# Two batches' forward transform kept on chip by transposes, and the second batch written ahead of the expert blocks

## The chip, the cores and the metric

One core of one Trainium2 chip. The metric is the device time of one execution in microseconds. PE is the tensor engine, DVE the vector engine, ACT the scalar engine, POOL the GpSimd engine; SP issues the plain DMAs from one queue, POOL the indirect ones.

## What is computed

Each of 8 batches (2496 x 256) is filtered along its length by a product in the frequency domain. The result, 19968 tokens of 256 numbers, goes through a mixture of 8 experts, each token to the two with the highest noisy logits.

```python
X = np.fft.rfft(x, axis=1)
y = np.fft.irfft(X * (filt_r + 1j * filt_i), n=2496, axis=1)      # x: 8 x 2496 x 256
x = y.reshape(19968, 256)
noisy = x @ w_gate + np.log1p(np.exp(x @ w_noise)) * noise        # 19968 x 8
# top 2 per token; weights = softmax of the two
out[mask] += w[mask, k, None] * (np.maximum(x[mask] @ w1[e], 0) @ w2[e])   # w1: 256 x 1024
```

## The kernel before

The length 2496 is split as 39 x 64, so that both transforms are small products with constant matrices. A batch has 22 groups of rows; a half-batch (n = 0 to 15) is one batch at 128 of the 256 channels. The steps, each with its function:

- `s1l` loads two groups of x (234 KB). `s1` multiplies by the 39-point matrix (`rC`, line 247: one f32 product of 512 columns for the first batches). `s1e` copies the result `c1` and writes it to memory, `fd` (line 264).
- `kgl` reads `fd` back as `fx` with frequency on the partitions (line 271, two DMAs of 128 KB for each of five groups `kg` of a half-batch). `kg0` passes it on or splits it into a high and a low part. `kg1` multiplies by the 64-point matrix (`rM`, line 292) and then by the filter (`fr`, `fi`; lines 302 to 305, four DVE instructions). `kg2` is the inverse 64-point product (line 316) and its copy into `G`.
- `logit_half` (line 328), `logits`, `gating` and the generator `gate` work out the gates, and with them, for each token, the place in the experts' lists (DVE, with small pieces on POOL).
- `t3` transposes `G` (line 379), `i2` does the inverse 39-point product (lines 394 to 396, three products of a split operand) and writes the tokens to `y` in memory (line 400).
- `route` writes the token numbers to the experts' lists, 44 indirect DMAs of POOL per batch (line 685).
- An expert block of 512 tokens reads its list (`lt`, line 703), gathers tokens (`xg`, line 722), loads and splits weights (`wst`, lines 753, 776, 777), turns the tokens (`turn`, line 736) and does both products (lines 113 to 115 into `hps` and `yps`); POOL adds the result to the output (line 835).

`load_filter` brings half of `fr` or `fi`, in four pieces over the prelude; every filter row is wanted twice, on partitions 0 to 63 and 64 to 127, and is loaded by a DMA with a broadcast leading dimension:

```python
t[:, h, k].rearrange("p k d -> p (k d)"),
io[nm][:, h, k].rearrange("b k d -> b (k d)").unsqueeze(0).to_broadcast([2, QB, n])
```

`sign` then multiplies `fi` by a table on POOL (line 205). `setup2` loads the remaining constants, `init_dram` and `zero_out` clear lists and output.

The order of the work: `fft_stream` is a generator that writes the transform of all batches; at each `yield` it may be left. It first writes batch 0 to its gates, then the inverse of batch 0 with the first stage of batch 1, and from n = 2 on, half-batch by half-batch, the forward steps X of n beside the inverse steps Y of n - 1. A yielded number says which batch is routed. `run` takes the stream to the first routed batch, then writes expert blocks and lets the stream advance in step with them (`PACE`), 2 blocks with batch 0 and 6 with batch 1. A scheduler reorders what has been written by a timing model, engine by engine. While `early` holds, the transform borrows the experts' buffers (tags such as `hh`, `wst`, `w1h`) and PSUM banks (`EARLY`).

Of the kernel before, what the change touches and what calls it, by code (L numbers as in the profile page):

```python
# [20 lines left out]
QA, QB = 39, 64  # L21
# [37 lines left out]
def _tables():  # L59
# [48 lines left out]
    sgn = np.concatenate([sg, -sg], 0).astype(np.float32)  # L108
    return dict(cf=cf, cm=np.ascontiguousarray(big[:, :248]).astype(np.float32), hl=hl, kf=kf, sgn=sgn, tok=tok, ok=tb < QB, small=small, lin=lin)

# [13 lines left out]
LEAD = 6  # L124
EARLY = {"q1": ("hps", 2), "q5": ("yps", 2), "q6": ("yps", 2), "u1": ("xps", 1)}


class Moe:
# [18 lines left out]
    def setup(self):  # L147
        tc, nc, io, cp = self.tc, self.nc, self.io, self.cp
        self.z = cp.tile([128, D], F32, name="z")
        nc.gpsimd.memset(self.z, 0.0)  # L150
        self.ident = cp.tile([128, 128], F32, name="ident")
        make_identity(nc, self.ident)
        self.cV = cp.tile([128, 128], F32, name="cf")
        hl = cp.tile([128, 732], R32, name="hl")
        self.small = cp.tile([128, 512], F32, name="small")
        self.fr = cp.tile([128, 2, 20, 128], F32, name="fr")
        self.fi = cp.tile([128, 2, 20, 128], F32, name="fi")
        self.wg = cp.tile([128, 2, 32], F32, name="wg")
        self.sgn = cp.tile([128, 20], F32, name="sgn")
        cm = self.P.tile([128, 248], F32, name="cm", tag="mxh0", bufs=1)  # L160
        nc.sync.dma_start(cm[:, 0:120], io["cm"][:, 0:120])
        with self.after(self.s1l(0, 0)):
            nc.sync.dma_start(cm[:, 120:248], io["cm"][:, 120:248])
        nc.sync.dma_start(self.cV, io["cf"])
        nc.sync.dma_start(self.sgn, io["sgn"])
        self.rC, self.rM = cm[:RP, 0:120], cm[:, 120:248]
# [12 lines left out]
        self.nblk = cp.tile([E, 1], F32, name="nblk")  # L179
        for t in (self.cnt, self.done, self.nblk):  # L180
            nc.vector.memset(t, 0.0)
        self.tab = cp.tile([1, 2, SW], F32, name="tab")

    def setup2(self):
        nc, io, hl = self.nc, self.io, self.hl
        for a in range(0, 732, 366):
            t = self.P.tile([128, 366], F32, name="cl", tag="fx", bufs=2)
            nc.sync.dma_start(t, io["hl"][:, a:a + 366])
            nc.scalar.copy(hl[:, a:a + 366], t)
        nc.sync.dma_start(self.small, io["small"])  # L190
        nc.sync.dma_start(self.wg[:, :, 0:16], io["wgn"])
        nc.vector.tensor_copy(self.base, self.eoff)

    def load_filter(self, h, a, b):
        nc, io = self.nc, self.io
        k, n = slice(4 * a, 4 * b), 512 * (b - a)
        for t, nm in (self.fr, "fr"), (self.fi, "fi"):

            self.lastx = nc.sync.dma_start(
                t[:, h, k].rearrange("p k d -> p (k d)"),  # L200
                io[nm][:, h, k].rearrange("b k d -> b (k d)").unsqueeze(0).to_broadcast([2, QB, n]))

# [35 lines left out]
    def s1(self, bt, g0):  # L238
# [19 lines left out]
        self.s1e(bt, g0, q)  # L258

    def s1e(self, bt, g0, q):  # L260
        nc, P, early = self.nc, self.P, self.early
# [24 lines left out]
    def kg1(self, n, kg):  # L286
# [6 lines left out]
        else:  # L293
            nc.tensor.matmul(p, Mh, th, start=True, stop=False)
            nc.tensor.matmul(p, Mh, tl, start=False, stop=False)
            nc.tensor.matmul(p, Ml, th, start=False, stop=True)
        a = P.tile([128, 4, 128], F32, name="a", **(dict(tag="wst", bufs=4) if self.early else dict(bufs=2)))
        b = P.tile([128, 4, 128], F32, name="b", bufs=1)
        p3 = p.rearrange("p (k d) -> p k d", k=4)
# [4 lines left out]
        nc.vector.tensor_mul(b[64:128], p3[0:64], fi[0:64])  # L304
        nc.vector.tensor_add(a, a, b)
        self.zz[n, kg] = a
# [66 lines left out]
    def t3(self, n, g0):  # L373
# [6 lines left out]
        m = 128 * k  # L380
        th = P.tile([128, 512], R32, name="th", **(dict(tag="w1h", bufs=4) if self.early else dict(bufs=3)))
        tl = P.tile([128, 512], R32, name="tl", **(dict(tag="w1l", bufs=4) if self.early else dict(bufs=3)))
        nc.scalar.copy(th[:120, :m], q[:120, :m])
# [3 lines left out]
    def i2(self, n, g0):  # L387
# [5 lines left out]
        p = self.ps("q6")  # L393
        nc.tensor.matmul(p[:RP, :m], Dh, th[:120, :m], start=True, stop=False)
        nc.tensor.matmul(p[:RP, :m], Dh, tl[:120, :m], start=False, stop=False)
        nc.tensor.matmul(p[:RP, :m], Dl, th[:120, :m], start=False, stop=True)
        yt = P.tile([RP, 4, 128], F32, name="yt", **(dict(tag=("mxl0", "mxh1", "mxl1")[g0 // 4 % 3], bufs=1) if self.early else dict(bufs=2)))
# [4 lines left out]
    def fft_stream(self):  # L402
# [10 lines left out]
        def s1(j):  # L413
            ahead(min(j + 5, 11) if j < 11 else j + 5 if self.early else j + 2)
            self.s1(*todo[j])

# [12 lines left out]

        more(self.load_filter, 0, 0, 2)  # L430
        q = [(n, kg) for n in range(2) for kg in range(5)]
        for t in range(13):
            if t < 10:
                self.kgl(*q[t])
                self.sign(*q[t])
            if t == 0:
                more(self.load_filter, 0, 2, 5)
            if t == 3:
                more(self.load_filter, 1, 0, 2)
                more(self.setup2)  # L440
            if t == 5:
                more(self.load_filter, 1, 2, 5)
            if t == 8:
                ahead(15)
            if 2 <= t < 12:
                self.kg0(*q[t - 2])
                self.kg1(*q[t - 2])
            if t >= 3:
                self.kg2(*q[t - 3])
            if t == 9:  # L450
                self.logit_half(0, 0)
# [24 lines left out]
        self.i2(1, gs[5])  # L476
        for i in range(4):
            more(self.zero_out, 0, i)
        for _ in range(4):
            self.gating_more(0)  # L480
        yield -1
        ns = 22
        route = self.route(0, *self.routes.pop(0))
        for n in range(2, N + 1):
            X = []
# [11 lines left out]
            if m >= 2:  # L497
                Y += [f(self.logit_half, m, 0), f(self.logit_half, m, 1)]
                T = [f(self.t3, m, g) for g in gs]
                I = [f(self.i2, m, g) for g in gs]  # L500
                if m % 2:
                    Y += [f(self.logits, 0), f(self.logits, 1), T[0], f(self.gating, m // 2)]
# [13 lines left out]
            for t in range(tot):  # L516
                while ix < len(X) and ix * tot <= t * len(X):
                    X[ix]()
                    ix += 1
                    if n == 2:  # L520
                        next(route, None)
                    yield -1
# [183 lines left out]
    def front(self, blk, xg):  # L706
# [3 lines left out]
        with self.after(self.spw):  # L710
            re = nc.sync.value_load(tabi[0:1, 1, s:s + 1], min_val=0, max_val=E - 1)
        w1st, w2st = self.load_w(re, "w1", nt), self.load_w(re, "w2", nt)
        w1 = [self.wsplit(w1st[q], "w1", q) for q in range(4)]
        return w1, self.turn(xg, nt), w2st

    def gather(self, blk, i):
# [3 lines left out]
        for t in range(nt):  # L720
            x = self.P.tile([128, D], F32, name="xg", bufs=8)
            self.nc.gpsimd.indirect_dma_start(  # L722
# [22 lines left out]
    def load_w(self, re, nm, nt):  # L745
# [3 lines left out]
        if nt == BLK // 128:  # L749
            r = []  # L750
            for q in range(4):
                t = P.tile([128, 1, 512], F32, name="wst", bufs=4)
                self.spw = nc.sync.dma_start(t, src[:, q].rearrange("e p f -> p e f"))
                r.append(t[:, 0])
            return r
        self.wodd = 1 - self.wodd if nm == "w1" else self.wodd
        if nm == "w2" and self.wodd:
            r = [P.tile([128, 1, 512], F32, name="wst", bufs=4) for _ in range(4)]
            for q in range(4):
                self.spw = nc.sync.dma_start(r[q], src[:, q].rearrange("e p f -> p e f"))  # L760
            return [t[:, 0] for t in r]
        if nm == "w2":
# [24 lines left out]
    def expert(self, parts, may):  # L787
# [5 lines left out]
        while self.ahead:  # L793
# [32 lines left out]
            for t in range(nt):  # L826
                p = self.PS.tile([128, D], F32, name="yps", bufs=2)
                for f in range(8):
# [3 lines left out]
                         start=(f == 0), stop=(f == 7))  # L832
                o = P.tile([128, D], F32, name="yo", bufs=6)
                nc.scalar.activation(o, p, AF.Copy, scale=gate[:, t, 1:2])  # L834
# [107 lines left out]
```

## Time and profile before

| | |
|---|---|
| median of 3 runs | 2489.76 us (2489.31 to 2491.03) |
| the profiled execution | 2490.21 us, its span 2488.3 us |
| PE busy | 2252.4 us, 91% of the span |
| VectorE, ScalarE, GpSimd busy | 1319.8, 1202.2, 1235.0 us |
| mean granted PE clock | 0.953 |

PE busy counts the time in which at least one matmul is under way; the granted clock is the share of full speed that PE was given. The rows of instructions in order of time give the start, the length, the engine (with a q where its queue issues a DMA), the line, output <- inputs, the count, and in brackets the idle time before and what ended it. The rows of a stretch give busy time (and instructions) of each engine, the granted clock, the mean busy share of the 16 DMA engines and what they moved.

### The profile page before, as it was taken

Reading aid. Unit: us, or ns where it says so; the run is one execution under the profiler, and the core shown is the slowest. Engines: PE = TensorE matmul, PEld = TensorE weight load, DVE = VectorE, ACT = ScalarE, POOL = GpSimd, SP = SyncE. Lnnn points to the kernel's source line nnn. Section 1 sums busy time; section 2 is a strip of 40 time slices with the busy share of each in tenths; the row PEclk is TensorE's granted clock in tenths of the full one; section 3 lists DMA queues with packets and bytes.
Section 4 is the critical chain, followed back from the end, with each engine's and each line's share of the span. In section 5 each row is a group of like instructions: output and inputs, shape, how many; then the busy total and the mean of one; then the engine's idle time right before and its main releaser. Section 6 shows DMA issues by size and latency. Waiting matters only on the chain.

```text
span 2488.3 us, 41972 instructions
## 1 busy us (share of the span) xinstructions
PE 2252.4 (91%) x14769; PEld 1974.4 (79%) x14769; DVE 1319.8 (53%) x2567; ACT 1202.2 (48%) x2274; POOL 1235.0 (50%) x1065
## 2 busy tenths in 40 slices
PE   2265796998998999999998999999999999999998
PEld 0133575887887888888887899989889989999998
DVE  0237775776666667576643434334334334456775
ACT  1144564564555555555543434344344344456775
POOL 0005375574574346533665467657744444444442
PEclk6687898999999999999998999999999999999999
DMA  4274657766656565455343443443444444558774
GB/s 137 78 226 133 184 130 196 185 154 166 154 125 164 139 152 146 114 150 148 92 91 77 95 94 78 105 91 86 97 91 96 90 92 94 137 139 221 227 236 99
DMA packets 300288, 330.34 MB, mean 133 GB/s; under 512 B 48310, under 2 KB 215598, under 8 KB 300072
## 3 DMA queue, kind: packets, MB, share of 16 engines
q1 hardware_dynamic: 227368, 243.30, 32.4%
q0 software_dynamic: 72704, 84.31, 20.3%
q8 instruction: 118, 1.93, 0.3%
q14 instruction: 98, 0.80, 0.1%
HBM read 220.33 MB, written 108.43 MB: 132 GB/s over the span
## 4 chain that ended last, share of the span: by engine, by line
PE 63%; DMA 2%; POOL 2%; DVE 2%; issue 1%; ACT 1%; SPq 0%; ACTq 0%; POOLq 0%; DVEq 0%
PE yps L113 9%; PE yps L115 9%; PE yps L114 9%; PE hps L113 9%; PE hps L114 9%; PE hps L115 9%; PE xps L736 2%; PE q L316 1%; POOL lst L685 1%; PE hq L115 1%; PE hq L114 1%; PE hq L113 1%; PE q L379 1%; POOL out L835 1%; DMA fd<-c 0%
## 5 line engine op out<-in xcount | busy, mean ns | idle before, releaser
L814 DVE SCALAR_TENSOR_TENSOR hl<-hps,hh 128x512 fp32r<-128x512 f32 (+1 forms) x640 | 417.0, 656 | 564.3 <-ACT hh L813 561.7
L113 PE MATMUL yps<-w2h,hh 128*128 128x256 f32 x2560 | 701.8, 284 | 2.6 <-ACT hh L813 2.6
L835 POOL DMA_INDIRECT out<-yo,lt x320 | 521.6, 1630 | 337.2 <-ACT yo L834 255.6
L114 PE MATMUL yps<-w2l,hh 128*128 128x256 f32 x2560 | 686.3, 278 | 0.0
L115 PE MATMUL yps<-w2h,hl 128*128 128x256 f32 x2560 | 632.0, 279 | 0.7 <-DVE hl L814 0.7
L722 POOL DMA_INDIRECT xg<-y,lt x320 | 324.2, 1013 | 562.8 <-PE xps L736 407.2
L813 ACT ACTIVATE hh<-hps 128x512 fp32r<-128x512 f32 (+1 forms) x640 | 363.1, 574 | 319.6 <-PE hps L115 314.5
L115 PEld LDWEIGHTS yps<-w2h,hl 128*128 128x128 f32 x2560 | 471.5, 188 | 35.5 <-DVE hl L814 1.2
L113 PEld LDWEIGHTS yps<-w2h,hh 128*128 128x128 f32 x2560 | 483.1, 189 | 16.3 <-ACT hh L813 4.7
L113 PE MATMUL hps<-mxh,w1h 128*128 128x512 f32 (+1 forms) x1280 | 486.3, 389 | 9.0 <-DVE hl L814 6.7
L114 PE MATMUL hps<-mxl,w1h 128*128 128x512 f32 (+1 forms) x1280 | 493.8, 386 | 0.0
L114 PEld LDWEIGHTS yps<-w2l,hh 128*128 128x128 f32 x2560 | 482.2, 188 | 7.8
L115 PE MATMUL hps<-mxh,w1l 128*128 128x512 f32 (+1 forms) x1280 | 487.6, 381 | 0.0
L685 POOL DMA_INDIRECT lst<-pay,dst x352 | 363.3, 1032 | 110.0 <-issue 103.4
L834 ACT ACTIVATE yo<-yps,lt 128x256 f32<-128x256 f32 x320 | 142.8, 475 | 338.8 <-PE yps L115 173.6
L115 PEld LDWEIGHTS hps<-mxh,w1l 128*128 128x128 f32 x1280 | 241.0, 188 | 46.6
L113 PEld LDWEIGHTS hps<-mxh,w1h 128*128 128x128 f32 x1280 | 240.7, 189 | 44.7 <-DVE hl L814 13.0
L114 PEld LDWEIGHTS hps<-mxl,w1h 128*128 128x128 f32 x1280 | 241.8, 189 | 24.8
L777 DVE TENSOR_TENSOR w1l<-wst,w1h 128x512 fp32r<-128x512 f32 x172 | 118.2, 687 | 103.9 <-ACT w1h L776 103.5
L776 ACT CAST w1h<-wst 128x512 fp32r<-128x512 f32 x172 | 106.4, 620 | 126.7 <-PE hps L114 74.7
L777 DVE TENSOR_TENSOR w2l<-wst,w2h 128x512 fp32r<-128x512 f32 x208 | 135.4, 687 | 56.3 <-ACT w2h L776 55.7
L740 ACT CAST mxh<-xps 128x512 fp32r<-128x512 f32 (+1 forms) x178 | 97.2, 546 | 129.2 <-PE xps L736 80.3
(165 smaller groups left out, 2579.0 us busy)
## 6 DMA issues: line engine op xcount, KB each, us to landing
wst<-w SPq DMA_DIRECT2D x380, 256.0 KB
fd<-c SPq DMA_DIRECT2D x88, 240.0 KB
x<-x SPq DMA_DIRECT2D x88, 234.0 KB
fx<-fd SPq DMA_DIRECT2D x160, 128.0 KB
y<-yt SPq DMA_DIRECT2D x80, 234.0 KB
wb<-w SPq DMA_DIRECT2D x18, 1024.0 KB
out<-z SPq DMA_DIRECT2D x24, 702.0 KB
wc<-w SPq DMA_DIRECT2D x36, 256.0 KB
```

The costliest lines, as they stand in the source:

```text
L113: nc.tensor.matmul(o, lh, rh, start=start, stop=False)
L114: nc.tensor.matmul(o, lh, rl, start=False, stop=False)
L115: nc.tensor.matmul(o, ll, rh, start=False, stop=stop)
L685: s = nc.gpsimd.indirect_dma_start(out=self.lst, out_offset=bass.IndirectOffsetOnAxis(ap=dst[:n, i, g:g + 1], axis=0), in_=pay[:n, g, i], ...
L722: self.nc.gpsimd.indirect_dma_start(out=x, out_offset=None, in_=self.y[:BLK + ready * ROWS], in_offset=bass.IndirectOffsetOnAxis(ap=lt[:, ...
L740: nc.scalar.copy(h, q[:, :w])
L776: nc.scalar.copy(h, sv)
L777: nc.vector.tensor_sub(l, sv, f32v(h))
L813: nc.scalar.activation(h, p, AF.Relu)
L814: nc.vector.scalar_tensor_tensor(l, p, 0.0, f32v(h), op0=ALU.max, op1=ALU.subtract)
L834: nc.scalar.activation(o, p, AF.Copy, scale=gate[:, t, 1:2])
L835: a = nc.gpsimd.indirect_dma_start(out=self.io["out"][:BLK + ready * ROWS], out_offset=bass.IndirectOffsetOnAxis(ap=ids[:, t, 0:1], axis=0 ...
```

## The change

The first stage of batches 0 and 1 (`s1c`) makes x the stationary operand, so that the result has channels on the partitions, and keeps it in SBUF as `F`, one array per half of the channels. `kgc` takes the place of `kgl` and `kg0`: four PE transposes and a copy by ACT. `fd` is not written or read for these batches. Each filter load becomes two DMAs of 64 partitions, and all of them and `setup2` are written ahead of the first `kgc`. For n < 2 the addition of line 305 goes to POOL. While `early` holds, `t3` makes one f32 copy and `i2` one f32 product with an unsplit matrix (`rD`).

In the stream, after batch 0's inverse, the forward steps of n = 2 and 3 are written with the first stage of batch 2 and `route(0)`, then the inverse of n = 2 and the whole gating of batch 1, and only then comes the first yielded batch; the loop over n starts at 4. `F` shares its 22.5 KB per partition (`stage`) with the experts' `wst`, `xg` and `yo`, which are now slots of this one tile, in turn (`slot`), 4, 8 and 6 as before. In `front` w2's loads are written after w1's splits.

```diff
-EARLY = {"q1": ("hps", 2), "q5": ("yps", 2), ...
+EARLY = {"q1": ("hps", 2), "q2": ("hps", 2), "q5": ("yps", 2), ...
+        self.stage = cp.tile([128, 5632], F32, name="stage")
+        self.F = [self.stage[:, 2560 * h:2560 * h + 2560].rearrange("p (k b) -> p k b", k=CB) for h in range(2)]
+    def slot(self, nm):
+        at, n, w = {"wst": (0, 4, 512), "xg": (2048, 8, 256), "yo": (4096, 6, 256)}[nm]
+        i = self.turns[nm] = (self.turns.get(nm, -1) + 1) % n
+        return self.stage[:, at + w * i:at + w * i + w]
...
-            self.lastx = nc.sync.dma_start(
-                t[:, h, k].rearrange("p k d -> p (k d)"),
-                io[nm][:, h, k].rearrange("b k d -> b (k d)").unsqueeze(0).to_broadcast([2, QB, n]))
+            src = io[nm][:, h, k].rearrange("b k d -> b (k d)")
+            for r in range(2):
+                self.lastx = nc.sync.dma_start(t[64 * r:64 * r + 64, h, k].rearrange("p k d -> p (k d)"), src)
...
+    def s1c(self, bt, j):
+        x = self.xx.pop((bt, 2 * j))
+        if j % 2 == 0:
+            self.sq = [self.ps("q1") for _ in range(2)]
+        for h in range(2):
+            q = self.sq[h][:, :12 * CB].rearrange("p (k b) -> p k b", b=12)
+            for i in range(2):
+                o, n = 6 * (j % 2) + 3 * i, 3 if 2 * j + i < NG - 1 else 1
+                nc.tensor.matmul(q[:, :, o:o + n].rearrange("p k b -> p b k"), x[:, i * D + h * 128:i * D + h * 128 + 128],
+                                 self.rC[:, :n * CB], start=True, stop=True)
+            if j % 2 or j == 10:
+                n = 12 if j % 2 else 4
+                (nc.vector.tensor_copy if h else nc.scalar.copy)(self.F[h][:, :, 12 * (j // 2):12 * (j // 2) + n], q[:, :, :n])
+    def kgc(self, n, kg):
+        q = self.ps("q2")
+        for j in range(4):
+            nc.tensor.transpose(q[:, j * 128:j * 128 + 128],
+                                F[:, 8 * kg + 2 * j:8 * kg + 2 * j + 2].rearrange("p r b -> p (r b)"), self.ident)
+        f = self.P.tile([128, 512], F32, name="fx", tag="hl", bufs=8)
+        nc.scalar.copy(f, q)
+        self.tt[n, kg] = f, None
...
-        nc.vector.tensor_add(a, a, b)
+        (nc.gpsimd if n < 2 else nc.vector).tensor_add(a, a, b)
...
+        if tl is None:
+            nc.tensor.matmul(p[:RP, :m], self.rD, th[:120, :m], start=True, stop=True)
...
+        for a in (0, 0, 2), (0, 2, 5), (1, 0, 2), (1, 2, 5):
+            more(self.load_filter, *a)
+        more(self.setup2)
...
+        route = self.route(0, *self.routes.pop(0))
+        Y = [f(self.logit_half, 2, 0), f(self.logit_half, 2, 1), f(self.t3, 2, gs[0])]
+        for t in range(12):
+            if t < 10:
+                self.kgc(*q[10 + t])
+            if 1 <= t < 11:
+                self.kg1(*q[10 + t - 1])
+            if t >= 2:
+                self.kg2(*q[10 + t - 2])
+            for _ in range(4):
+                next(route, None)
+            if t < 11:
+                s1(22 + t)
+            if t < 4:
+                more(self.zero_out, 0, t)
+            for _ in range(3 if t >= 7 else 0):
+                if Y:
+                    Y.pop(0)()
+        self.logit_half(3, 0)
+        self.logit_half(3, 1)
+        self.logits(0)
+        self.logits(1)
+        self.gating(1)
...
+        for _ in range(10):
+            self.gating_more(1)
+        ns = 33
+        yield 0
+        for n in range(4, N + 1):
```

More of the change, by code (lines that the diff above doesn't have):

```diff
@@ L124 @@
 LEAD = 6
-EARLY = {"q1": ("hps", 2), "q5": ("yps", 2), "q6": ("yps", 2), "u1": ("xps", 1)}
+EARLY = {"q1": ("hps", 2), "q2": ("hps", 2), "q5": ("yps", 2), "q6": ("yps", 2), "u1": ("xps", 1)}
 class Moe:
@@ L296, in kg1 @@
             nc.tensor.matmul(p, Ml, th, start=False, stop=True)
-        a = P.tile([128, 4, 128], F32, name="a", **(dict(tag="wst", bufs=4) if self.early else dict(bufs=2)))
-        b = P.tile([128, 4, 128], F32, name="b", bufs=1)
+        a = P.tile([128, 4, 128], F32, name="a", **(dict(tag="w2h", bufs=4) if self.early else dict(bufs=2)))
+        b = P.tile([128, 4, 128], F32, name="b", **(dict(tag="w2l", bufs=4) if self.early else dict(bufs=1)))
         p3 = p.rearrange("p (k d) -> p k d", k=4)
@@ L380, in t3 @@
         m = 128 * k
-        th = P.tile([128, 512], R32, name="th", **(dict(tag="w1h", bufs=4) if self.early else dict(bufs=3)))
-        tl = P.tile([128, 512], R32, name="tl", **(dict(tag="w1l", bufs=4) if self.early else dict(bufs=3)))
+        if self.early:
+            t = P.tile([128, 512], F32, name="tf", tag="w1h", bufs=4)
+            nc.scalar.copy(t[:120, :m], q[:120, :m])
+            self.t3t[n, g0] = t, None
+            return
+        th = P.tile([128, 512], R32, name="th", bufs=3)
+        tl = P.tile([128, 512], R32, name="tl", bufs=3)
         nc.scalar.copy(th[:120, :m], q[:120, :m])
@@ L414, in s1 @@
             ahead(min(j + 5, 11) if j < 11 else j + 5 if self.early else j + 2)
-            self.s1(*todo[j])
+            if j < 22:
+                self.s1c(j // 11, j % 11)
+            else:
+                self.s1(*todo[j])
         def ahead(to):
@@ L428, in fft_stream @@
             yield -1
-        more(self.load_filter, 0, 0, 2)
-        q = [(n, kg) for n in range(2) for kg in range(5)]
-        for t in range(13):
+        q = [(n, kg) for n in range(4) for kg in range(5)]
+        for a in (0, 0, 2), (0, 2, 5), (1, 0, 2), (1, 2, 5):
+            more(self.load_filter, *a)
+        more(self.setup2)
+        for t in range(12):
             if t < 10:
-                self.kgl(*q[t])
+                self.kgc(*q[t])
                 self.sign(*q[t])
[L436 to L442, printed above, removed]
-            if t == 8:
[L444 to L450, printed above, removed]
+            if t == 7:
+                ahead(15)
+            if 1 <= t < 11:
+                self.kg1(*q[t - 1])
+            if t >= 2:
+                self.kg2(*q[t - 2])
+            if t == 8:
                 self.logit_half(0, 0)
@@ L476, in fft_stream @@
         self.i2(1, gs[5])
-        for i in range(4):
-            more(self.zero_out, 0, i)
         for _ in range(4):
@@ L519, in fft_stream @@
                     ix += 1
-                    if n == 2:
-                        next(route, None)
                     yield -1
@@ L720, in gather @@
         for t in range(nt):
-            x = self.P.tile([128, D], F32, name="xg", bufs=8)
+            x = self.slot("xg")
             self.nc.gpsimd.indirect_dma_start(
@@ L751, in load_w @@
             for q in range(4):
-                t = P.tile([128, 1, 512], F32, name="wst", bufs=4)
-                self.spw = nc.sync.dma_start(t, src[:, q].rearrange("e p f -> p e f"))
-                r.append(t[:, 0])
+                t = self.slot("wst")
+                self.spw = nc.sync.dma_start(t.unsqueeze(1), src[:, q].rearrange("e p f -> p e f"))
+                r.append(t)
             return r
@@ L757, in load_w @@
         if nm == "w2" and self.wodd:
-            r = [P.tile([128, 1, 512], F32, name="wst", bufs=4) for _ in range(4)]
+            r = [self.slot("wst") for _ in range(4)]
             for q in range(4):
-                self.spw = nc.sync.dma_start(r[q], src[:, q].rearrange("e p f -> p e f"))
-            return [t[:, 0] for t in r]
+                self.spw = nc.sync.dma_start(r[q].unsqueeze(1), src[:, q].rearrange("e p f -> p e f"))
+            return r
         if nm == "w2":
@@ L832, in expert @@
                          start=(f == 0), stop=(f == 7))
-                o = P.tile([128, D], F32, name="yo", bufs=6)
+                o = self.slot("yo")
                 nc.scalar.activation(o, p, AF.Copy, scale=gate[:, t, 1:2])
```

40 lines of the change are left out of this document (28 added, 12 removed).

## The prediction, made before the result was known

> **What bounds the kernel now.** I read the page's strip of 40 slices first, then one table of busy time by stretch whose cuts I chose after reading the order of instructions in time, then that order itself for the vector, DMA and tensor queues around the cuts.
>
> ```profile
> span 2488.3 us, 41972 instructions
> PE   2265796998998999999998999999999999999998
> core 0: us, PE busy (x) PEld busy (x) DVE busy (x) ACT busy (x) POOL busy (x), PEclk, DMA share, GB/s
> 0.00:20.00 20.00, 12.82 (x22) 4.07 (x22) 0.37 (x8) 7.72 (x12) 1.15 (x9) 1.00 0.81 261
> 20.00:136.00 116.00, 16.95 (x52) 10.05 (x52) 16.78 (x28) 6.66 (x7) 7.11 (x8) 0.56 0.24 80
> 136.00:170.00 34.00, 30.80 (x141) 16.18 (x141) 15.17 (x23) 19.14 (x31) 3.19 (x4) 0.89 0.82 247
> 170.00:206.00 36.00, 17.87 (x75) 10.26 (x72) 19.50 (x74) 13.62 (x28) 1.88 (x7) 0.75 0.88 268
> 206.00:264.00 58.00, 37.23 (x190) 24.53 (x194) 38.50 (x64) 27.07 (x41) 44.90 (x44) 0.82 0.36 91
> 264.00:282.00 18.00, 10.07 (x42) 5.71 (x32) 10.38 (x22) 10.48 (x22) 8.25 (x10) 0.69 0.86 264
> 282.00:372.00 90.00, 84.25 (x514) 70.07 (x514) 71.24 (x160) 54.99 (x95) 47.77 (x48) 0.97 0.52 141
> 372.00:402.00 30.00, 9.08 (x51) 5.97 (x50) 7.01 (x13) 6.04 (x10) 20.64 (x20) 0.60 0.61 146
> 402.00:2488.30 2086.30, 2033.36 (x13695) 1827.54 (x13695) 1140.85 (x2179) 1056.48 (x2031) 1100.12 (x919) 0.99 0.53 130
> ```
>
> From 402 us on, PE is busy for 2033.36 of 2086.30 us: what reaches that point earlier ends earlier, one for one. Ahead of it PE idles for 183 of 402 us. The worst stretch is 20 to 136: PE busy 16.95 of 116 us, and the DMA engines at 0.24 of their time, 80 GB/s, though 261 and 268 GB/s are reached on either side. So something slow on few engines is being waited for, not bandwidth:
>
> ```profile
> 20.06 0.74 SPq L199 DMA_DIRECT2D fr<-fr  x1
> 39.90 33.41 SPq L271 DMA_DIRECT2D fx<-fd  x6
> 44.50 2.04 POOL L205 TENSOR_TENSOR fi<-fi,sgn 128x512 f32<-128x512 f32 x2 [42.76 <-DMA fi<-fi]
> 135.99 3.03 POOL L205 TENSOR_TENSOR fi<-fi,sgn 128x512 f32<-128x512 f32 x3 [33.57 <-DMA fi<-fi]
> L205 POOL TENSOR_TENSOR fi<-fi,sgn 128x512 f32<-128x512 f32 x10 | 10.1, 1038 | 127.1 <-DMA fi<-fi 127.1
> ```
>
> The first 1 MB of filters (fr and fi, 512 KB each) is issued at 20.06 and lets the sign product go only at 44.50: 24 us. The last quarter is there at 135.99. Behind each filter load in SP's one queue stand the reads fx<-fd, six of which take 33.41 us to issue. The filter loads, with the trip of the spectrum through memory between them, set this stretch. After it a chain runs whose ends the next rows give:
>
> ```profile
> 169.46 0.81 PE L328 MATMUL u<-G,wg 128*32 128x360 f32 x8
> 205.74 1.19 POOL L685 DMA_INDIRECT lst<-pay,dst  x1 [3.03 <-DVE en L651]
> 263.28 0.89 POOL L685 DMA_INDIRECT lst<-pay,dst  x1 [0.30 <-issue]
> 281.56 1.22 PE L113 MATMUL hps<-mxh,w1h 128*128 128x512 f32 x2 [1.01 <-ACT mxh L740]
> 262.59 2.62 PE L328 MATMUL u<-G,wg 128*32 128x360 f32 x16 [4.59 <-ACT G L317]
> 314.72 1.02 POOL L685 DMA_INDIRECT lst<-pay,dst  x1 [0.31 <-DVE new L650]
> 378.69 0.90 POOL L685 DMA_INDIRECT lst<-pay,dst  x1 [0.30 <-issue]
> 391.77 0.48 PE L736 MATMUL xps<-ident,xg 128*128 128x128 f32 x1 [18.48 <-DMA xg<-y,lt]
> ```
>
> First batch: last logits of the spectrum 169.46, gates, 44 scatters of the route 205.74 to 264.2 on POOL, lists and gathers, first expert matmul 281.56. That is 112.1 us from logits to expert. Second batch: logits 262.59, route 314.72 to 379.6, and PE has nothing for 18.48 us because the gathers wait for it.
>
> **The change part by part.** The instruction prices, at full clock unless said:
>
> ```profile
> 7.35 10.78 PE L247 MATMUL q<-x,cm 117*120 117x512 f32 x20 [0.63 <-DMA x<-x]
> 79.46 1.91 PE L316 MATMUL q<-cf,a 128*128 128x128 f32 x8
> 82.67 1.13 PE L316 MATMUL q<-cf,a 128*128 128x128 f32 x8
> 83.64 1.02 PE L292 MATMUL q<-fx,cm 128*128 128x512 f32 x2
> 151.21 0.60 PE L379 MATMUL q<-ident,G 128*120 128x128 f32 x4
> 183.72 1.10 PE L379 MATMUL q<-ident,G 128*120 128x128 f32 x4 [2.52 <-DVE tl L384]
> 149.57 0.48 PE L394 MATMUL q<-th,hl 120*117 120x512 f32 x1
> 150.12 0.39 PE L396 MATMUL q<-th,hl 120*117 120x512 f32 x1
> L263 ACT COPY c<-q 120x512 f32<-120x512 f32 x46 | 27.1, 589 | 46.5 <-PE q L247 46.2 <-ACT th L383 0.3
> L317 ACT COPY G<-q 128x512 f32<-128x512 f32 x30 | 34.8, 1159 | 96.1 <-PE q L316 96.1
> L302 DVE TENSOR_TENSOR a<-q,fr 128x512 f32<-128x512 f32 x30 | 20.6, 686 | 110.4 <-PE q L292 107.8 <-PE q L296 2.0
> fd<-c SPq DMA_DIRECT2D x88, 240.0 KB
> ```
>
> *First stage (s1c).* One f32 product of 512 columns per pair of groups (10.78 us for ten) becomes four of 120 columns; nearest row L316, four f32 products of 128 columns in 1.13. Eleven make 12.4 us. Two PSUM banks are filled by two steps and then copied, one by ACT and one by DVE (0.59 by L263): the next pair waits about 0.6 us, five times, 3 us. Begun at about 5 us, the first two at half clock (1.91), it ends at 22 us, against 18 now. The writes fd<-c go, and their places in SP's queue.
>
> *Filter loads.* Each broadcast becomes two plain loads of 64 partitions, 16 issues of some 0.5 us, and none has an fx read ahead of it: they follow the last x load, about 15 us. They move 5.24 MB (fr and fi, 128 x 5120 f32 each). Their new rate stands in no row of that form; bounds are 80 GB/s (the stretch 20 to 136) and 261 (0 to 20). I take 261, since x<-x too is a plain load of one row per partition: 20 us, landing from about 19 to 37 us, the quarters in the order in which they are used. At 80 GB/s the last lands at 81. The Trainium skill, "DMA: Bandwidth & Descriptors", section "Why a DMA increments its semaphore by 16 and not by 1", says that a transfer is spread over the largest number of engines up to 16 that divides the slowest dimension of both sides: that is 2 for a broadcast whose outer dimension is 2, and 16 for 64 rows. The low share of 0.24 agrees; by the rule the sum is the one I take, and by the rate of the present loads it is rival A's.
>
> *Spectrum of the first batch (kgc, kg1, kg2).* Ten groups, each on PE four transposes (0.60), a product (1.02), eight instructions of L316 (1.13): 2.75 us. The chain of one group is the product, three DVE products (3 x 0.686), the addition, now on POOL (1.04 like L205's), then kg2; with one other group between in PE's order that sets about 3.1 us a group. ACT needs 0.59 + 1.16, POOL 2.08 with the sign product: both fit. Ten groups 31 us and 3 for the first to fill: logits at 56 instead of 169.46, **113.5 us sooner**. Bounds: 50 us (PE alone, 2.75), and 93 with the slow filters.
>
> *Gates, route, gathers of the first batch.* No instruction of it changes: 112.1 us, of which 58.4 are POOL's scatters. First expert at 168. Beside it PE now has the second batch's s1c (12.4), inverse of three half-batches (18 t3 groups, 9.9; 16.5 products of 1.02, 16.8), ten groups of 2.75 (27.5), eleven s1 (11.2) and logits, 5: 83 us in 112, where the table shows 65 busy in 170 to 282. So the transposes and the f32 product in i2 (1.02 for 0.94) cost nothing while this chain covers them; uncovered, ten times 0.60, eleven s1c at +0.05 and 17 products at +0.08 cost 8 us. zero_out, init_dram and the first y writes go past SP in this stretch; at 247 to 268 GB/s there is room, since 22 of the fd writes (5.4 MB) and as much read back as fx are gone.
>
> *Second batch's gates ahead of all blocks.* In the present kernel these gates are written between the instructions of the first blocks, and 52 us pass from logits (262.59) to the first scatter (314.72); the first batch needs 36.3. I keep the logits 19 us ahead of the first expert, as now, and take 36 to 39: the route begins 13 us sooner, and the 18.48 us wait shrinks by **13 us**. Bounds: the wait goes whole, 18.5, or grows by 10 if POOL's out additions are served first. If this wait goes, PE itself is next.
>
> *Steady part.* wst, xg and yo become slots of one tile with as many places as their pools; w2's loads are written after w1's splits, whose slots they need anyway. I take 0, bounds -10 and +10, a fifth of the 53 us that PE idles after 402.
>
> Sum against the profiled execution, 2490.2 us (span 2488.3 and 1.9 around it): 2490.2 - 113.5 - 13 = 2363.7. The median of the runs shown is 0.4 lower, so **2364**.
>
> **The rivals.** *A, filters stay slow.* The last quarter lands at 81 (80 GB/s) where the eighth group asks for it at 22 + 7 x 3.1 = 44: 37 us more, 2401. The broadcast is gone, which speaks against it.
>
> *B, cold clock and a longer chain.* PE's granted clock was 0.56 in the idle stretch and 0.82 in 206 to 264. If it stays near half through the prelude, a group costs 1.10 + 2.04 + 1.91 = 5 us, 19 us more over ten, and the 83 us beside the route become 150 or so, over 112 by some 30: about 2410. For it: four transposes took 1.10 at 183.72 after a wait. Against it: the 0.60 of others at 151.21, amid dense work. The Trainium skill, "TensorE: Matmul & The Clock Gate", section "Part 4: PE-mode transpose", says that the full clock does not engage for transposes, which would speak against adding 80 of them; the 0.60 contradicts it where products stand beside them.
>
> *C, slower.* Slots of one tile could be ordered as one thing: a weight load would wait for the last reader of any slot.
>
> ```profile
> L835 POOL DMA_INDIRECT out<-yo,lt x320 | 521.6, 1630 | 337.2 <-ACT yo L834 255.6
> 47.67 0.69 DVE L302 TENSOR_TENSOR a<-q,fr 128x512 f32<-128x512 f32 x1 [46.47 <-PE q L292]
> 73.35 0.54 SPq L199 DMA_DIRECT2D fr<-fr  x1
> ```
>
> There are 320/4 = 80 blocks; from 126.5/80 = 1.6 us a block it eats the gain, and with one addition's 1.63 us per token tile (four a block) it costs 521, a time of 2885. Against it: the product at 47.67 read a part of fr before another part's load was issued at 73.35, so parts are ordered apart.
>
> *D, no change.* The first expert sooner, but every microsecond handed back as waits for the second batch's lists: about 2490. Against it, that its forward work has 29 us of PE to spare above.
>
> **How the numbers follow.** Forecast 0.65 (2330 to 2395), A 0.08, B 0.18, C 0.05, D 0.04. Range 2330 to 2418: it takes in A and most of B, and the forecast's bounds (50 instead of 56, all of the wait, 10 in the steady part: 2342; a little more for a shorter chain). About 0.2% (5 us) is what the measurement can tell from no change: faster 0.91, same 0.03, slower 0.06.
>
> **What would show it.** Right: sign products released by 40 us, the logits at about 56, POOL's first scatter at 92, first expert at 168, the second wait under 8 us, PE nearly full after. Wrong: DMA share below 0.4 between 20 and 60 (A); granted clock below 0.8 between 20 and 150 (B); waits of weight loads on gathers or additions (C); PE idle for tens of microseconds ahead of the second batch's blocks (D).

## The result and the profile after

The changed kernel takes 2402.65 us (median of 4 runs, 2401.66 to 2403.85), the kernel before beside it 2490.4 (2489.31 to 2491.68): a ratio of 0.965 (95% interval 0.9637 to 0.9662), 88 us less. The forecast was 2364 in a range of 2330 to 2418: faster, and 39 us too low. The forecast's own span ended at 2395; the time lies in the part of the range that was added for the rivals A and B. The profiled execution took 2401.66 us, its span is 2399.9.

The table of stretches of the changed kernel, cut at its own landmarks (first expert 200, second batch's lists 262), in the columns of the table of before:

```profile
20.00:44.00 24.00, 15.30 (x72) 10.27 (x71) 8.91 (x16) 9.22 (x15) 12.59 (x13) 0.86 0.98 249
44.00:80.00 36.00, 35.82 (x246) 26.36 (x246) 17.84 (x28) 21.94 (x34) 10.23 (x9) 1.00 0.70 221
80.00:112.00 32.00, 21.86 (x92) 11.98 (x89) 16.32 (x70) 15.82 (x32) 2.08 (x7) 0.82 0.73 220
112.00:170.00 58.00, 41.05 (x200) 23.25 (x200) 39.19 (x79) 28.95 (x45) 44.90 (x44) 0.85 0.32 84
170.00:201.00 31.00, 15.71 (x59) 11.19 (x60) 19.55 (x64) 10.62 (x19) 18.16 (x24) 0.63 0.54 165
201.00:262.00 61.00, 57.82 (x356) 48.87 (x354) 43.21 (x69) 38.52 (x69) 46.08 (x42) 0.99 0.57 137
262.00:282.00 20.00, 16.65 (x103) 14.83 (x104) 11.05 (x17) 10.95 (x21) 14.21 (x13) 0.85 0.90 268
282.00:2399.90 2117.90, 2067.93 (x13749) 1861.98 (x13747) 1146.62 (x2187) 1061.29 (x2036) 1103.31 (x919) 0.99 0.53 128
```

The stretch with 80 GB/s and a DMA share of 0.24 is gone: 0.98 and 249 GB/s stand in its place, and PE is full by 44 us. What PE idles ahead of the second batch's blocks has shrunk from 183 us to 65. But the last stretch holds a surprise: 2067.93 us of PE work are left, where before 2033.36 were left at 402 us.

The rows in order of time that answer to those shown of before:

```profile
23.94 2.04 POOL L216 TENSOR_TENSOR fi<-fi,sgn 128x512 f32<-128x512 f32 x2 [22.19 <-DMA fi<-fi]
31.38 3.03 POOL L216 TENSOR_TENSOR fi<-fi,sgn 128x512 f32<-128x512 f32 x3 [5.41 <-DMA fi<-fi]
34.37 2.48 POOL L343 TENSOR_TENSOR a<-a,b 128x512 f32<-128x512 f32 x2
35.69 2.07 PE L354 MATMUL q<-cf,a 128*128 128x128 f32 x8 [4.83 <-POOL a L343]
40.91 3.03 POOL L216 TENSOR_TENSOR fi<-fi,sgn 128x512 f32<-128x512 f32 x3 [2.06 <-DMA fi<-fi]
79.36 0.81 PE L366 MATMUL u<-G,wg 128*32 128x360 f32 x8
111.58 1.19 POOL L760 DMA_INDIRECT lst<-pay,dst  x1 [3.04 <-DVE done L739]
175.38 0.33 SPq L620 DMA_DIRECT2D noise<-noise  x1
181.09 1.73 SPq L778 DMA_DIRECT2D lt<-lst  x2
200.37 0.74 PE L113 MATMUL hps<-mxh,w1h 128*128 128x512 f32 x2 [0.22 <-ACT mxh L816]
258.24 6.55 SPq L778 DMA_DIRECT2D lt<-lst  x6
263.68 0.48 PE L812 MATMUL xps<-ident,stage 128*128 128x128 f32 x1 [4.68 <-DMA stage<-y,lt]
391.71 1.59 POOL L911 DMA_INDIRECT out<-stage,lt  x1 [0.30 <-ACT hh L889]
2322.17 1.60 POOL L911 DMA_INDIRECT out<-stage,lt  x1 [0.30 <-ACT w1h L852]
```

The last two rows are the 20th and the 308th of the 320 additions to the output, two posts at which both kernels have the same expert blocks behind them. The same posts of the kernel before:

```profile
504.32 2.00 POOL L835 DMA_INDIRECT out<-yo,lt  x1 [0.30 <-ACT th L282]
...
2412.09 1.59 POOL L835 DMA_INDIRECT out<-yo,lt  x1 [0.30 <-ACT w1h L776]
```

At the 20th the changed kernel is 112.6 us ahead, at the 308th 89.9. So the 39 us between forecast and result have two parts: 14 missing at the start (126.5 were forecast), and about 23 lost slowly afterwards. The costliest groups show who loses it, of before first and then of after (busy us, mean ns of one):

```profile
L113 PE MATMUL yps<-w2h,hh 128*128 128x256 f32 x2560 | 701.8, 284 | 2.6 <-ACT hh L813 2.6
L114 PE MATMUL yps<-w2l,hh 128*128 128x256 f32 x2560 | 686.3, 278 | 0.0
L115 PE MATMUL yps<-w2h,hl 128*128 128x256 f32 x2560 | 632.0, 279 | 0.7 <-DVE hl L814 0.7
```

```profile
L113 PE MATMUL yps<-w2h,hh 128*128 128x256 f32 x2560 | 713.9, 288 | 15.5 <-ACT hh L889 15.4
L114 PE MATMUL yps<-w2l,hh 128*128 128x256 f32 x2560 | 701.5, 283 | 0.0
L115 PE MATMUL yps<-w2h,hl 128*128 128x256 f32 x2560 | 640.4, 282 | 0.7 <-DVE hl L890 0.7
```

The same 7680 matmuls of the second expert product are busy 2055.8 instead of 2020.1 us: 35.7 more, which covers the 34.6 more that the last stretch holds. The first product (hps) did not change. From start to start of neighbouring yps matmuls, over blocks 12 to 76 and without the gaps above 160 ns, the mean is 119.0 ns instead of 114.9, at a granted clock of 0.99 in both last stretches.

### The profile page after: what moved, and what is told of

The parts are those of the page before. It is cut to its first block, busy times and chain, and to the rows that moved or that the text cites. A ratio compares the mean times of both kernels' runs of the same rounds, so it can differ in the third digit from the quotient of the medians.

```text
span 2399.9 us, 42183 instructions
## 1 busy us (share of the span) xinstructions
PE 2285.2 (95%) x14951; PEld 2021.2 (84%) x14951; DVE 1306.3 (54%) x2539; ACT 1201.4 (50%) x2274; POOL 1252.7 (52%) x1075
## 4 chain that ended last, share of the span: by engine, by line
PE 78%; DMA 4%; POOL 3%; issue 3%; DVE 2%; ACT 2%; SPq 1%; DVEq 0%; ACTq 0%; POOLq 0%
PE yps L113 11%; PE yps L115 11%; PE yps L114 11%; PE hps L113 11%; PE hps L114 10%; PE hps L115 10%; PE xps L812 3%; POOL lst L760 2%; PE q L354 2%; PE q L417 1%; DMA fx<-fd 1%; DMA stage<-w 1%; POOL out L911 1%; PE u L366 1%; PE hq L115 1%
## 5 line engine op out<-in xcount | busy, mean ns | idle before, releaser
L113 PE MATMUL yps<-w2h,hh 128*128 128x256 f32 x2560 | 713.9, 288 | 15.5 <-ACT hh L889 15.4
L114 PE MATMUL yps<-w2l,hh 128*128 128x256 f32 x2560 | 701.5, 283 | 0.0
L911 POOL DMA_INDIRECT out<-stage,lt x320 | 523.1, 1635 | 336.6 <-ACT stage L910 254.5
L115 PE MATMUL yps<-w2h,hl 128*128 128x256 f32 x2560 | 640.4, 282 | 0.7 <-DVE hl L890 0.7
L798 POOL DMA_INDIRECT stage<-y,lt x320 | 325.3, 1017 | 557.1 <-PE xps L812 405.8
L115 PEld LDWEIGHTS yps<-w2h,hl 128*128 128x128 f32 x2560 | 476.7, 190 | 35.3 <-DVE hl L890 1.2
L910 ACT ACTIVATE stage<-yps,lt 128x256 f32<-128x256 f32 x320 | 142.7, 474 | 339.5 <-PE yps L115 176.3
L853 DVE TENSOR_TENSOR w1l<-stage,w1h 128x512 fp32r<-128x512 f32 x172 | 118.0, 687 | 96.9 <-ACT w1h L852 96.5
L853 DVE TENSOR_TENSOR w2l<-stage,w2h 128x512 fp32r<-128x512 f32 x208 | 136.2, 689 | 61.2 <-ACT w2h L852 60.1
L852 ACT CAST w1h<-stage 128x512 fp32r<-128x512 f32 x172 | 106.5, 619 | 115.3 <-PE hps L114 77.8
```

Source lines behind the costliest of these rows:

```text
L113: nc.tensor.matmul(o, lh, rh, start=start, stop=False)
L114: nc.tensor.matmul(o, lh, rl, start=False, stop=False)
L115: nc.tensor.matmul(o, ll, rh, start=False, stop=stop)
L798: self.nc.gpsimd.indirect_dma_start(out=x, out_offset=None, in_=self.y[:BLK + ready * ROWS], in_offset=bass.IndirectOffsetOnAxis(ap=lt[:, ...
L852: nc.scalar.copy(h, sv)
L853: nc.vector.tensor_sub(l, sv, f32v(h))
```

## The experiments

The first four kernels ran on one chip, beside the kernel before at 2489.01 us. On the chips of the later eight that kernel took 2646 to 2649 us, so these are read against it and against one another only.

### e1_filters and e2_bcast: which part earns the gain

`e1_filters` is the kernel before with nothing but the filter loads changed; `e2_bcast` is the changed kernel with the broadcast loads back.

```diff
 # e1_filters, from before (e2_bcast: the reverse, from after)
-            self.lastx = nc.sync.dma_start(t[:, h, k]..., io[nm][:, h, k]....unsqueeze(0).to_broadcast([2, QB, n]))
+            for r in range(2):
+                self.lastx = nc.sync.dma_start(t[64 * r:64 * r + 64, h, k]..., src)
```

> The kernel before with nothing changed but the filter loads: two plain loads of 64 partitions for each broadcast. Theory 1 (the broadcast loads run on few engines and hold SP's queue and the sign products; they are the larger part of the gain): the last sign product by about 60 instead of 136 us, the first batch's last logits 60 to 80 us sooner than 169, total about 2490 - 70 = 2420. Rival (the trip of the spectrum through fd and fx is what the stretch 20 to 136 waits for): less than 25 us, 2465 or more.

> The changed kernel with the broadcast filter loads put back. Theory 1: filters land at the old rate, last quarter near 90 us, the first batch's logits 35 to 55 us later than 79; total about 2402 + 45 = 2447. Rival (on-chip transposes alone carry the gain): within 10 us of 2402.

Measured: e1_filters 2409.72 us, ratio 0.9679 (0.966 to 0.9698). e2_bcast 2487.3, ratio 0.9992 (0.9981 to 1.0002). Rows of e1_filters in order of time:

```profile
27.77 2.04 POOL L205 TENSOR_TENSOR fi<-fi,sgn 128x512 f32<-128x512 f32 x2 [26.03 <-DMA fi<-fi]
...
56.25 3.03 POOL L205 TENSOR_TENSOR fi<-fi,sgn 128x512 f32<-128x512 f32 x3 [10.08 <-DMA fi<-fi]
...
90.00 0.81 PE L328 MATMUL u<-G,wg 128*32 128x360 f32 x8
...
125.56 1.19 POOL L685 DMA_INDIRECT lst<-pay,dst  x1 [3.02 <-DVE en L651]
...
203.68 1.22 PE L113 MATMUL hps<-mxh,w1h 128*128 128x512 f32 x2 [2.14 <-ACT mxh L740]
```

The stretch 20 to 60 in e1_filters and then in e2_bcast:

```profile
20.00:60.00 40.00, 17.07 (x54) 9.29 (x54) 18.32 (x31) 6.67 (x7) 10.13 (x10) 0.69 1.07 242
```

```profile
20.00:60.00 40.00, 6.64 (x40) 4.25 (x38) 4.13 (x6) 5.45 (x10) 2.03 (x2) 0.65 0.13 53
```

The three edited lines alone bring the last sign product from 136 to 56 us, the first batch's last logits from 169.46 to 90.00 and the time down by 79 us. All the rest of the change, with the slow loads, brings 1.7 us, which the interval cannot tell from nothing. The trip of the spectrum through memory was not what mainly held the prelude; the loads in front of it in the queue were. With the trip gone too, in the changed kernel, the logits come at 79.36, 11 us sooner still, but the first expert only 3 us sooner (200.37 against 203.68). In e2_bcast no read of the spectrum stands between the filter loads in the queue, and yet the engines move 53 GB/s at a share of 0.13: it is the form of the load. That is the rule of the Trainium skill ("DMA: Bandwidth & Descriptors", section "Why a DMA increments its semaphore by 16 and not by 1") by which an outer dimension of 2 confines a transfer to 2 engines; a share of 2/16 is 0.125, and the trace agrees with 0.13.

My expectation of 2447 for e2_bcast was 40 us too low, because the loads cost more than I took: the last sign products come at 115.80, not near 90, and the first batch's last logits at 156.67, 77 us behind the changed kernel's and not 35 to 55. The run shows a second thing. It is 28 us ahead of the kernel before at the 20th addition (476.46 against 504.32) and 5.5 at the 308th (2406.62): its yps matmuls are as slow as the changed kernel's (713.5, 701.2 and 640.7 us), those of e1_filters as fast as those of before (701.3, 685.7, 632.0). So the slow loss comes with the rest of the change.

### e3_layout: where the operands lie in SBUF

In the prelude of the changed kernel the buffers `a` and `b` borrow the tags `w2h` and `w2l`. The tiles are laid out in the order in which the tags first appear, so w2's halves lie at 118 to 135 KB of a partition and not at 196 to 213 KB. `e3_layout` lets `a` and `b` borrow other tags, and w2 goes to 185 to 201 KB.

```diff
-        a = P.tile(..., **(dict(tag="w2h", bufs=4) if self.early else dict(bufs=2)))
-        b = P.tile(..., **(dict(tag="w2l", bufs=4) if self.early else dict(bufs=1)))
+        a = P.tile(..., **(dict(tag="w1l", bufs=4) if self.early else dict(bufs=2)))
+        b = P.tile(..., **(dict(tag="tl", bufs=3) if self.early else dict(bufs=1)))
```

> The changed kernel; in the prelude the buffers a and b borrow the places w1l and tl in place of w2h and w2l, so that w2h and w2l get other addresses in SBUF (185 to 201 KB in place of 118 to 135 KB); nothing else differs. The second product of the experts (yps) goes at 119.0 ns a matmul in the changed kernel and at 114.9 in the one before, which is 18 to 26 us over the steady part. Theory A (it is the place of its operands in SBUF): the pace returns to about 115 ns, total about 2402 - 22 = 2380. Theory B (it comes from the slots of one tile, or from w2's loads written after w1's splits): pace stays at 119, total 2400 to 2405.

Measured: 2377.81 us, ratio 0.9546 (0.9527 to 0.9564), 25 us less than the changed kernel. Its groups, and then its two posts:

```profile
L113 PE MATMUL yps<-w2h,hh 128*128 128x256 f32 x2560 | 703.0, 284 | 19.6 <-ACT hh L889 19.6
L114 PE MATMUL yps<-w2l,hh 128*128 128x256 f32 x2560 | 688.8, 279 | 0.2 <-DVE w2l L853 0.2
L115 PE MATMUL yps<-w2h,hl 128*128 128x256 f32 x2560 | 632.8, 280 | 0.8 <-DVE hl L890 0.8
```

```profile
395.41 1.59 POOL L911 DMA_INDIRECT out<-stage,lt  x1 [0.30 <-ACT ut L372]
...
2307.68 1.60 POOL L911 DMA_INDIRECT out<-stage,lt  x1 [0.30 <-ACT w1h L852]
```

31.2 us of the 35.7 are back, and the pace is 115.05 ns from start to start. The lead is 108.9 us at the first post and 104.4 at the second: all but 4.5 us of it are kept, where the changed kernel lost 22.7. The slots, the order of writing and the places of `hh` and `hl` (82 to 118 KB) are the same as in the changed kernel, so they are not what slows the blocks; w2's place is.

### e5_low_before: the place alone, in the kernel before

```diff
 # from before
-        a = P.tile(..., **(dict(tag="wst", bufs=4) if self.early else dict(bufs=2)))
-        b = P.tile(..., name="b", bufs=1)
+        a = P.tile(..., **(dict(tag="w2h", bufs=4) if self.early else dict(bufs=2)))
+        b = P.tile(..., name="b", **(dict(tag="w2l", bufs=4) if self.early else dict(bufs=1)))
```

> The kernel before, with only the prelude's borrowed buffers a and b on the tags w2h and w2l, as the change has them, so that w2's halves move from about 196 to 92 KB per partition in SBUF, between hh and hl; nothing of the transform, its loads or its order is changed. Theory A (the place of yps's operands in SBUF sets the pace of the matmuls): start to start of yps matmuls goes from 114.9 to about 119 ns in the blocks, PE busy over L113 to L115 by some 25 us more, the time 2505 to 2515. Rival (the change's slots and order of writing, not the place, slow the blocks): pace 114.9 as before, time 2485 to 2495.

Measured: 2670.76 us against 2649.41 of before, 21 us more, ratio 1.0072 (1.0047 to 1.0097). As the program lays the tiles out, w2 lies at 92 to 108 KB there, right behind `hl` (75 to 92 KB), and not between `hh` and `hl`. The kernel before has no trace on this chip; the nearest with w2 high is `e7_add_dve`. Groups of e5_low_before, then of e7_add_dve:

```profile
L113 PE MATMUL yps<-w2h,hh 128*128 128x256 f32 x2560 | 721.4, 290 | 60.7 <-ACT hh L813 46.2 <-issue 14.3
L114 PE MATMUL yps<-w2l,hh 128*128 128x256 f32 x2560 | 709.1, 286 | 3.7 <-issue 3.6
L115 PE MATMUL yps<-w2h,hl 128*128 128x256 f32 x2560 | 647.3, 285 | 9.0 <-issue 8.2 <-DVE hl L814 0.7
```

```profile
L113 PE MATMUL yps<-w2h,hh 128*128 128x256 f32 x2560 | 710.3, 287 | 41.2 <-ACT hh L889 33.1 <-issue 5.9 <-ACT stage L910 1.5
L114 PE MATMUL yps<-w2l,hh 128*128 128x256 f32 x2560 | 694.8, 281 | 1.5 <-issue 1.5
L115 PE MATMUL yps<-w2h,hl 128*128 128x256 f32 x2560 | 639.1, 282 | 2.6 <-issue 2.4
```

With w2 low these groups are busy 33.6 us more, and the pace is 119.2 ns from start to start, against 115.0 in e7_add_dve. `e7_add_dve` is a changed kernel, so it serves for the pace only; against the kernel before, nothing but two tags in the prelude differs, and the time is 21 us longer. The place of w2 in SBUF sets the pace, in both kernels and both ways.

### e4_lead1: the lists behind the second route

Between the end of the first route and the first expert lie 30.3 us, where before had 17.4. SP reads the lists at 181.09: it stood 17.3 us at the noise load of the second gates, which waits for DVE, and then 5.1 us for scatters of the second route that are written ahead of the reads (six steps, `LEAD`).

```diff
-LEAD = 6
+LEAD = 1
```

> The changed kernel with 1 instead of 6 steps of the stream written ahead of the first expert block, so that no scatter of the second batch's route is written ahead of the first batch's list reads. Theory (the first list reads wait for three scatters of the second route, and so for the second batch's gates): the lists are read some 3 us after the last scatter of the first route instead of 11, the first expert matmul about 8 to 12 us sooner than 200, total about 2393. Rival (the waiting is SP's queue behind the noise load, or is given back at the second batch's lists): total within 3 us of 2402.

Measured: 2411.99 us, ratio 0.9686 (0.967 to 0.9702), 9 us more than the changed kernel. Rows in order of time:

```profile
175.12 1.73 SPq L778 DMA_DIRECT2D lt<-lst  x2
187.65 1.22 PE L113 MATMUL hps<-mxh,w1h 128*128 128x512 f32 x2 [0.67 <-ACT mxh L816]
195.87 1.21 POOL L760 DMA_INDIRECT lst<-pay,dst  x1 [3.47 <-DVE dst L690]
...
264.02 6.17 SPq L778 DMA_DIRECT2D lt<-lst  x6
```

The mechanism is as said: the first expert comes 12.7 us sooner. But the noise load now comes at 192.94, the second route starts at 195.87 instead of 177.63, and the second lists are read 5.8 us later than 258.24. The gathers behind them keep PE waiting 8.79 us at 269.31, instead of 4.68, and at the 308th addition the kernel is 13.9 us behind the changed one (2336.11 against 2322.17). What the first block won, the second batch's blocks paid back, and more: the rival named the mechanism, but neither the theory's 2393 nor the rival's 2402 within 3 us came out. What makes up the rest of the loss was not tried. The path to the second lists counts as much as that to the first expert.

### e6_first_only and f2_first_only: the second batch not written ahead

Both are e3_layout with the second batch through memory and its steps among the first blocks, as before.

```diff
-            if j < 22:
+            if j < 11:
                 self.s1c(j // 11, j % 11)
...
-        for n in range(4, N + 1):
+        for n in range(2, N + 1):
```

> The changed kernel in the layout of e3_layout, but only the first batch's forward transform stays on chip; the second batch goes through memory and is written among the first blocks, as in the kernel before. Theory (of the 31 us between e1_filters and e3_layout most comes from the first batch's shorter path): first expert at 195 to 200, second wait of PE 15 to 20 us, time 2385 to 2395. Rival (it comes from the second batch being written ahead): first expert as in e1_filters, 200 to 204, time 2405 to 2412. Third possibility: the first expert comes sooner than in e3_layout since POOL's second route isn't ahead of the list reads, and nothing is lost behind, 2375 to 2380.

> The kernel of e3_layout once more, as the base that shares a chip with the next three. On a chip like the first: 2375 to 2382, ratio 0.955. Should this chip stall engines without a visible cause, as the one of e5_low_before to e8_raw4 did, only the ratios among these four are read.

> The kernel of e6_first_only beside its base. If writing the second batch ahead is what brings the change below e1_filters: 25 to 30 us above f1_layout. If the first batch's forward transform on chip brings it: within 8 us of f1_layout, first expert of both 195 to 205 us, second wait of PE 15 us or more in this kernel.

Measured: e6_first_only 2561.01 us, ratio 0.967 (0.9628 to 0.9712), without a base on its chip. On the next chip f1_layout took 2565.2, ratio 0.9674 (0.9642 to 0.9705), and f2_first_only 2563.73, ratio 0.9671 (0.9646 to 0.9695): no difference that the intervals, some 8 us either way, could tell. The first expert of f2_first_only comes at 220.9 and that of f1_layout at 238.8, and at the 20th addition they are 5.4 us apart the other way. On this chip writing the second batch ahead thus did not bring the 25 to 30 us. That what it saves at the second lists it costs at the first is not shown by this pair: ahead of its first expert f1_layout has 39 us of waits without a releaser, f2_first_only 32 (the last section shows the longest), and e3_layout, the same kernel on the first chip, has its first expert at 202.9. How the 32 us between e1_filters and e3_layout divide on the first chip was not tried.

### e7_add_dve, e8_raw4, f3_add_dve, f4_add_raw: two waits of the first batch

In the changed kernel POOL's additions (ten, those of the first batch's two half-batches) queue behind sign products that wait for a filter quarter: PE stands 4.83 us at 35.69 for an addition that POOL starts at 34.37, right behind the signs of 31.38. And DVE stands 6.51 us among the gates, at 100.70, for a copy of the fourth batch's split input.

```diff
 # e7_add_dve, f3_add_dve, f4_add_raw, from e3_layout
-        (nc.gpsimd if n < 2 else nc.vector).tensor_add(a, a, b)
+        nc.vector.tensor_add(a, a, b)
 # e8_raw4, f4_add_raw
-RAW = 3
+RAW = 4
```

> e3_layout with the addition of the first four half-batches on DVE again. Theory (POOL's in-order sign products, which wait for the filters, hold the additions and so the spectrum): logits of the first batch 4 to 6 us sooner than 79, first scatter as much sooner, time 2370 to 2376. Rival (DVE's three products a group leave no room for a fourth instruction, 0.69 us x 10): logits within 1 us of 79 or later, time 2377 to 2384.

> e3_layout with the first stage of the fourth batch too as one f32 product instead of a split one (RAW 4), which takes away the copies for which DVE waited 6.5 us among the first batch's gates. Theory (that wait is on the path to the first expert): first scatter 5 to 6 us sooner, time 2370 to 2374. Rival (POOL's 44 scatters and the list reads behind them set it, or PE's slower f32 product takes the gain): first scatter sooner by less than 2 us, or first expert unmoved, time 2376 to 2384.

> The kernel of e7_add_dve beside its base. In e7_add_dve the first scatter came at 108.1 where e3_layout had 115.2; if that moves the route, the lists and the end with it: 5 to 8 us below f1_layout. If the next thing (POOL's second route, the second batch's lists) takes it back: within 3 us of f1_layout.

> f3_add_dve with RAW 4. In e8_raw4 the first scatter came at 113.0, 2.2 us sooner than in e3_layout. If that adds: 2 us below f3_add_dve, first scatter at about 106. If PE's unsplit f32 products cost as much: equal to f3_add_dve or up to 5 us above.

Measured: e7_add_dve 2555.84 us, ratio 0.9642 (0.9603 to 0.9681); e8_raw4 2556.02, 0.9641 (0.9619 to 0.9663). Beside the base: f1_layout 0.9674 (0.9642 to 0.9705), f3_add_dve 2549.33, 0.9619 (0.9593 to 0.9645), f4_add_raw 2558.11, 0.9646 (0.9622 to 0.967). Rows of f1_layout, then of f3_add_dve:

```profile
34.33 2.08 PE L354 MATMUL q<-cf,a 128*128 128x128 f32 x8 [5.44 <-POOL a L343]
...
80.37 0.81 PE L366 MATMUL u<-G,wg 128*32 128x360 f32 x8
...
112.14 1.19 POOL L760 DMA_INDIRECT lst<-pay,dst  x1 [3.03 <-DVE new L725]
```

```profile
27.61 1.16 PE L354 MATMUL q<-cf,a 128*128 128x128 f32 x8 [0.48 <-DVE a L343]
...
44.33 2.06 PE L281 MATMUL q<-cm,x 117*128 117x120 f32 x8 [8.24 <-DMA x<-x]
...
76.59 0.81 PE L366 MATMUL u<-G,wg 128*32 128x360 f32 x8
...
109.21 1.19 POOL L760 DMA_INDIRECT lst<-pay,dst  x1 [2.88 <-DVE new L725]
```

With the addition on DVE the 5.44 us wait is gone and the first of these products comes 6.7 us sooner, but the logits only 3.8 us and the first scatter 2.9. The next thing in line takes the rest: at 44.33 PE waits 8.24 us for the second batch's x, where f1_layout waits 2.65, and SP issues these loads from 36.24 on, behind the filters and the constants. At the 308th addition f3_add_dve is 8.8 us ahead, and its median is 16 us lower. The two intervals still overlap a little, so the direction is likely and the size is not shown. RAW 4 adds nothing: the logits of f4_add_raw come at 79.5 and its first scatter at 112.7, and it is 9 us above f3_add_dve in the median. DVE's wait was off the path, or PE's unsplit products ate it. None of these four was run on the first chip, where e3_layout has the lowest time; f3_add_dve has the lowest of the later ones.

## Why the prediction was right, and where it was short

*Filter loads.* Right: 261 GB/s was taken, 249 came; the sign products were to be released by 40 us and the last was at 40.91. Rival A (2401) gives about the time measured, but by what did not happen: a DMA share of 0.98, not below 0.4. By the total alone one would have believed it.

*Spectrum of the first batch.* Mis-sized: logits at 79.4 instead of 56. Some 10 of the 23 us are gone before the first group's inverse product, which came at 35.69 where 22 and 3 to fill were taken. The addition on POOL was costed by its duration (1.04, in fact 1.27) and not by what stands ahead of it in POOL's queue, the sign products that wait for DMA: DVE had its part of the first group done at 26.84, and the addition started at 34.37. f3_add_dve shows that this wait can be had back, and that 4 us of it reach the logits. The rest comes later: the 3.1 us a group assumed that PE does nothing else, but PE was full from 44 to 80 (35.82 of 36), with the second batch's first stage and the first one's inverse put between the groups by the scheduler.

*Gates and route.* Right: 36.3 us to the first scatter were taken, 32.2 came; the 44 scatters took their 58.

*Route to first expert.* Missed by 13 us: "No instruction of it changes" overlooked what the change put in front of the list reads, the noise load in SP's queue and second-route scatters in POOL's. e4_lead1 shows that these us can be had back at the first expert, and that they are not free to take.

*The lead.* These two make the first expert 32 us late (200.4 for 168). Yet the lead was only 14 us short (112.6 for 126.5). What I had not counted is work moved ahead of the first expert: PE has 142.8 us of it behind it there, where before had 125.7, 17 us more though 81.2 us sooner. About 8 us of these, by my own working, are the change's additional products. At the second lists PE's idle time fell from 26.7 us (282 to 402) to 6.5 (201 to 282), 20.2 us. 81.2 + 17 - 8 + 20.2 make 110. That the start came out near the forecast is thus luck in part: the work moved ahead (17 - 8 = 9 us) and 7 us more idle time saved at the second lists than was taken (20.2 for 13) made up half of the 32 us that the two terms had lost, and neither was in the sum. The wait itself went from 18.48 to 4.68 us, 13.8 where 13 were forecast.

*Steady part.* (The sum as written gives 2363.3, not 2364, a slip of no weight.) The step that failed: 0 was taken with bounds of 10 either way. It is some 23 us, and e3_layout and e5_low_before show why. The bound came from PE's idle time after 402, and so from the assumption that a matmul of unchanged shape has an unchanged price; in fact w2's move in SBUF took the pace from 114.9 to 119.0 ns.

*Rivals.* B's clock was 0.82 to 1.00 from 20 to 112 us, so not cold; single groups of products behind a wait were slow (2.07 us at 35.69, where 1.13 was taken). The rule cited there from "TensorE: Matmul & The Clock Gate" of the Trainium skill didn't decide anything: the stretch 44 to 80, with transposes among the products, ran at 1.00. C is out, the slots order as parts: where SP waits ahead of the loads into `stage`, the trace names no gather and no addition, and the longest wait in total, for the split of w1 on DVE, is 804.6 us against 791.0 before. D is out in the changed kernel, but it is what e4_lead1 shows in small: time won at the first expert and handed back behind the second lists.

## What to carry to other kernels

Look first at a low DMA share next to a long wait: three lines that split a broadcast load into two plain ones earned 79 of the 88 us, and the large restructuring around it nearly nothing until its side effect was found. When buffers borrow each other's tags, compare the mean time of the unchanged instructions before and after; a shift of under 2% in the busy time of the largest groups can eat a gain made elsewhere. Time won on the path to the first block counts only as far as the path to the next batch's lists moves with it.

## What the runs showed of the hardware

The pace of these f32 matmuls with 256 moving columns hangs on where w2, the moving operand, lies in SBUF: 119.0 ns from start to start with w2 at 118 to 135 KB of a partition and 119.2 at 92 to 108 KB, but 115.05 at 185 to 201 KB and 114.9 at 196 KB and up; the weight loads of the same product took 190 ns instead of 188 to 189 on average. The cause is open. In e3_layout w1l lies at 118 to 127 KB, and the hps matmuls that read it keep their 394 ns; but there w1l is the operand that is loaded as weights and not the moving one, so this does not decide whether the place alone is enough. In both slow layouts w2 begins where `hl` ends. Whether it is this nearness to the other operand, or another access to the same part of SBUF, was not tried. The Trainium skill, "SBUF — State Buffer", section "SBUF: two separate sides", says that PE never waits on anyone at its ports; no run here shows a port at fault, but the price is not independent of the place.

The same kernel took 2377.81 us on one chip and 2565.2 on another. Among the waits of f1_layout between 120 and 215 us stand some of a kind that e3_layout does not have there:

```profile
ACT G L355 <- remote: 32.3, 2, 17.7
```

These are two waits of together 32.3 us, the longer of 17.7, for which the trace shows no releaser; DVE has one more of 7.0. The first expert is at 238.8 there and at 202.9 on the first chip. They are not the whole of the 187 us: over the execution PE idles 243.8 us in f1_layout against 120.9 in e3_layout, and is busy 53.9 us longer. What held the engines is open.
